# The last network's second quarter by seven block products, and a weight conversion whose stores and refills leave its list of steps

## The chip, the core and the metric

The kernel runs on one core of a Trainium2 chip. Its metric is the device time of one execution in microseconds, the median of several. A core has five engines with queues of their own: PE (TensorE, matrix products), DVE (VectorE), ACT (ScalarE), POOL (GpSimd) and SP (SyncE, which here only issues transfers). Each engine runs its own instructions strictly in the order in which they were recorded, and waits for another engine only where data or a buffer asks for it. So one instruction that waits holds up everything behind it on its engine.

## The reference, cut to what matters

```python
def reference(**inputs):
    # attention: 2 batches, 8 heads, 576 positions, 64 wide, causal window of 128, ALiBi slopes
    x = attention(q, k, v).reshape(1152, 512)
    # four experts, all dense, weighted by normalised probabilities
    p = domain_probs / (domain_probs.sum(-1, keepdims=True) + 1e-09)
    out = 0
    for e in range(4):                       # w1[e]: 512 x 1024, w2[e]: 1024 x 512
        out += p[:, e:e + 1] * (np.maximum(out_of_attention @ w1[e], 0) @ w2[e])
    # the last network: w_in 512 x 2048 and w_out 2048 x 512, both in float64
    h = np.maximum(out @ w_in, 0)
    return (h * h @ w_out).astype(np.float32)
```

`w_in` and `w_out` come as 64-bit floats, since they are drawn as float32 and multiplied by a float64 number.

## The kernel before, in words

**Arithmetic.** A value is kept as a rounded high part and a low part, the remainder, and a product of two such values is three matmuls (high by high, high by low, low by high). ACT makes the high parts by a copy, POOL or DVE the low parts by a subtraction (`rest`, L498 to L500).

**Networks.** The work is a sequence of six networks of 1024 hidden features: `e` = 0 to 3 are the experts (networks 1 to 4 in the text), `e` = 4 and 5 are the two halves of the last network. Each has four weight quarters `g` of 256 hidden features. The second half of `e` = 4, quarters 2 and 3, is the second quarter of the last network.

**Two forms of the first layer.** The plain form (`gemm1`) takes one feature tile `f` of 128 for a chunk of 384 tokens in 12 matmuls; four of them are followed by the second layer (`gemm2`) of that chunk. It is used by `e` = 0 and, before the change, by all of `e` = 4. The block form (`gemm1_pair`, L995 to L1120) takes a whole quarter: weights and tokens are cut into 2 x 2 blocks, and the four blocks of the result come from seven block products instead of eight, each of 2 x 3 matmuls, so 42 matmuls an item. Its token pairs are 2 x 256 (a narrow item, tokens 0 to 511) and 2 x 320 (a wide item, tokens 512 to 1151). Each half of a network runs narrow, narrow, wide, wide: two quarters for the first token pair, then for the second. The second layer of an item runs after the first layer of the next.

**Inside an item.** Three banks `pa`, `pb`, `pc` take the seven products. ACT copies `pa` to `p1` and `pc` to `p5`. DVE adds `u2 = pb + p1` after the second product and `u3 = pb + p1` after the fifth; both are called `u` in the trace, and the fifth and seventh products add into `pb` and so wait for them. DVE and ACT then make the four result blocks `c`, their high and low parts `hmem`.

**Forms.** The block form needs sums of blocks. For weights (`w_forms`, L342) POOL makes four sums (`wsum`, L356), three low parts of blocks (`la`) and four of sums (`ls`), 11 operations, where the plain form (`w_ops`) needs four (`wl`). For tokens (`x_forms`) DVE adds `fxwork` sums (L972).

**Results.** The second layer collects in up to five banks `yacc`. In networks 2 to 4 DVE adds each, scaled by a probability, to `y` (`evac`, L1182); a tile takes one DVE operation. After network 4, PE transposes the nine `y` tiles into the tokens of the last network (`to_x2`).

**Conversion.** DVE and ACT turn the 64-bit weights into 32-bit ones (`convert`, L226 to L312), in 32 halves. A half `j` has an ACT step (`begin`, L271) and four on DVE: a clamp (L277), a shift (L284) and two joins (L291). It works in one of two places `raw` and one of two halves of `both`; `swap` stores a finished half to DRAM (L251) and `reload` fills its place again (L239), both on ACT's queue and, before the change, both steps of the same list, in fixed positions.

**What sets the order.** The code is recorded in the order written. Between the products and tiles it calls `fill(share, us, need)` (L1323 on), which advances a planned clock and lets background steps in: token forms, up to three conversion steps, and weight steps by a quota. A conversion step on DVE goes in only if its planned end lies within `need` of the clock (`spare`), and a running allowance `conv_due` limits their number. So `need` is the opening that DVE's planned work may fill at that place. `want` forces what is overdue.

## Time and profile before

| | |
|---|---|
| median of 3 runs | 670.93 us (670.90 to 671.08) |
| profiled execution | 671.51 us |
| its span, first to last instruction | 669.7 us |
| PE busy | 657.0 us, 98% of the span |
| DVE, ACT, POOL busy | 473.1, 314.8, 395.6 us |
| granted PE clock, mean | 0.995 of full |

The span lies inside the profiled execution's own time, with 1.8 us around it; that execution took 0.58 us longer than the median. Attention and the first network fill the first 183 us, networks 2 to 4 run until about 461 us and the last one until the end. PE's busy time counts overlapping matmuls once; the start-to-start distance of matmuls, and not the duration of one, tells how fast they go.

### The profile page before, as it was taken

Reading aid. Unit: us, or ns where it says so; the run is one execution under the profiler, and the core shown is the slowest. Engines: PE = TensorE matmul, PEld = TensorE weight load, DVE = VectorE, ACT = ScalarE, POOL = GpSimd, SP = SyncE. Lnnn points to the kernel's source line nnn. Section 1 sums busy time; section 2 is a strip of 40 time slices with the busy share of each in tenths; the row PEclk is TensorE's granted clock in tenths of the full one; section 3 lists DMA queues with packets and bytes.
Section 4 is the critical chain, followed back from the end, with each engine's and each line's share of the span. In section 5 each row is a group of like instructions: output and inputs, shape, how many; then the busy total and the mean of one; then the engine's idle time right before and its main releaser. Section 6 shows DMA issues by size and latency. Waiting matters only on the chain.

```text
span 669.7 us, 10853 instructions
## 1 busy us (share of the span) xinstructions
PE 657.0 (98%) x3864; PEld 586.1 (88%) x3864; DVE 473.1 (71%) x982; ACT 314.8 (47%) x761; POOL 395.6 (59%) x473
## 2 busy tenths in 40 slices
PE   7999999999999999999999999999999999999997
PEld 6767888888989899898999989898999999898996
DVE  4787888847888777777877876876668744545453
ACT  5798888623435434333443343433464634333120
POOL 3799996526957744653654664231458984856321
PEclk8999999999999999999999999999999999999999
DMA  7943222011413443444345245354222001100012
GB/s 208 270 121 98 65 73 74 11 64 31 158 32 110 122 142 117 140 127 142 127 125 156 81 134 182 102 181 134 72 95 79 1 0 64 64 0 1 1 64 78
DMA packets 44023, 64.42 MB, mean 96 GB/s; under 512 B 4161, under 2 KB 26177, under 8 KB 43969
## 3 DMA queue, kind: packets, MB, share of 16 engines
q1 hardware_dynamic: 33248, 39.61, 19.4%
q10 hardware_dynamic: 10720, 24.12, 11.9%
q8 instruction: 30, 0.49, 0.3%
q14 instruction: 25, 0.20, 0.1%
HBM read 52.97 MB, written 10.75 MB: 95 GB/s over the span
## 4 chain that ended last, share of the span: by engine, by line
PE 91%; POOL 3%; DVE 2%; ACT 2%; SPq 1%; DMA 1%; issue 1%; POOLq 0%; ACTq 0%
PE yacc L1128 29%; PE hps L1050 26%; PE hps L936 14%; PE yacc L1163 13%; PE xps L731 3%; PE tp L859 2%; PE sc L811 2%; POOL wl L500 1%; PE hps L1575 1%; POOL ts L847 1%; DMA pt<-in_probs_dram 1%; SPq L1399 1%; POOL vl L500 1%; PE xtp L1198 1%; DVE fxwork L972 1%
## 5 line engine op out<-in xcount | busy, mean ns | idle before, releaser
L1128 PE MATMUL yacc<-wh,hmem 128*128 128x512 f32 x576 | 183.7, 390 | 0.0
L500 POOL TENSOR_TENSOR wl<-wraw,wh 128x256 fp32r<-128x256 f32 (+1 forms) x110 | 107.5, 1002 | 63.7 <-ACT wh L433 51.2
L1128 PEld LDWEIGHTS yacc<-wh,hmem 128*128 128x128 f32 x576 | 108.2, 188 | 21.8
L1128 PE MATMUL yacc<-wl,hmem 128*128 128x512 f32 x288 | 112.3, 390 | 0.0
L1163 PE MATMUL yacc<-wh,hmem 128*128 128x512 f32 x272 | 89.2, 393 | 0.0
L500 POOL TENSOR_TENSOR ls<-wsum,hs 128x256 fp32r<-128x256 f32 x64 | 54.5, 879 | 48.1 <-ACT hs L380 47.5
L1061 ACT ACTIVATE p<-hps 128x256 f32<-128x256 f32 (+1 forms) x64 | 26.3, 411 | 98.9 <-PE hps L1050 98.4
L936 PE MATMUL hps<-xh,wh 128*128 128x384 f32 (+1 forms) x208 | 67.1, 323 | 0.0
L936 PE MATMUL hps<-xh,wl 128*128 128x384 f32 (+1 forms) x208 | 65.5, 315 | 0.0
L936 PE MATMUL hps<-xl,wh 128*128 128x384 f32 (+1 forms) x208 | 65.4, 314 | 0.0
L1065 DVE TENSOR_TENSOR u<-hps,p 128x256 f32<-128x256 f32 (+1 forms) x64 | 29.1, 455 | 50.1 <-PE hps L1050 50.0
L1128 PEld LDWEIGHTS yacc<-wl,hmem 128*128 128x128 f32 x288 | 54.1, 188 | 9.9
L1163 PEld LDWEIGHTS yacc<-wh,hmem 128*128 128x128 f32 x272 | 51.0, 188 | 10.4
L291 DVE SCALAR_TENSOR_TENSOR wconv<-wraw,wconv 128x512 int32<-128x512 int32 x64 | 57.2, 894 | 1.3
L1085 ACT ACTIVATE hmem<-c 128x256 fp32r<-128x256 f32 (+1 forms) x72 | 31.0, 445 | 54.1 <-DVE c L1065 52.8
L847 POOL TENSOR_SCALAR ts<-ts,st 128x256 f32<-128x256 f32 (+2 forms) x80 | 40.6, 523 | 26.5 <-DVE st L842 12.3
L500 POOL TENSOR_TENSOR la<-wraw,ha 128x256 fp32r<-128x256 f32 x48 | 44.4, 950 | 19.7 <-ACT ha L366 19.7
L1163 PE MATMUL yacc<-wl,hmem 128*128 128x512 f32 x136 | 53.2, 391 | 0.0
L500 POOL TENSOR_TENSOR hmem<-c,hmem 128x256 fp32r<-128x256 f32 (+1 forms) x32 | 26.9, 861 | 38.3 <-ACT hmem L1081 38.3
L500 POOL TENSOR_TENSOR hmem<-r,hmem 128x384 fp32r<-128x384 f32 x24 | 26.2, 1094 | 39.0 <-ACT hmem L1150 39.0
L1086 DVE SCALAR_TENSOR_TENSOR hmem<-c,hmem 128x256 fp32r<-128x256 f32 (+1 forms) x72 | 38.6, 556 | 14.5 <-ACT hmem L1085 13.0
L832 ACT ACTIVATE ts<-ts,st 128x256 f32<-128x256 f32 (+2 forms) x80 | 37.2, 467 | 12.0 <-DVE st L823 12.0
(141 smaller groups left out, 1743.3 us busy)
## 6 DMA issues: line engine op xcount, KB each, us to landing
wraw<-in_w_dram SPq DMA_DIRECT2D x32, 512.0 KB, 4.1
wraw<-in_w_out_dram ACTq DMA_DIRECT2D x16, 512.0 KB, 3.8
w<-wconv ACTq DMA_DIRECT2D x32, 256.0 KB, 4.0
wraw<-w SPq DMA_DIRECT2D x16, 512.0 KB, 3.5
wraw<-in_w_in_dram ACTq DMA_DIRECT2D x14, 512.0 KB, 3.9
rq<-in_qT_dram SPq DMA_DIRECT2D x8, 256.0 KB, 7.1
out_dram<-y SPq DMA_DIRECT2D x8, 256.0 KB, 2.3
rk<-in_kT_dram SPq DMA_DIRECT2D x8, 192.0 KB, 5.7
```

Of the source, the lines that this page charges most:

```text
L291: nc.vector.scalar_tensor_tensor(out=ai, in0=raw[j][:, :, part], scalar=amount, in1=ai, op0=op, op1=ALU.bitwise_or,)
L500: e.tensor_tensor(out=out, in0=in0, in1=f32(in1), op=ALU.subtract)
L832: nc.scalar.activation(out=ts[0:n, g, :], in_=ts[0:n, g, :], func=ACTF.Exp, bias=st[0:n, 0, g:g + 1], scale=-1.0, accum_out=st[0:n, 1, g:g ...
L847: nc.gpsimd.tensor_scalar(out=ts[0:n, g, :], in0=ts[0:n, g, :], scalar1=st[0:n, 2, g:g + 1], scalar2=1.0, op0=ALU.mult, op1=ALU.mult,)
L936: nc.tensor.matmul(out=ps, lhsT=l_[:, k, cs], rhs=r_[:, k, cols], start=(k == 0 and r_ is xh and l_ is wh and not second), stop=(k == KT - ...
L1050: nc.tensor.matmul(out=ps, lhsT=a[l_][:, k, :], rhs=b[r_][:, k, :], start=start and k == 0 and l_ == r_, stop=stop and k == 1 and l_ == 1, ...
L1061: nc.scalar.activation(out=out, in_=x, func=ACTF.Copy)
L1065: nc.vector.tensor_tensor(out=out, in0=x, in1=y, op=ALU.add)
L1085: nc.scalar.activation(out=hh, in_=src, func=ACTF.Relu)
L1086: nc.vector.scalar_tensor_tensor(out=hl, in0=src, scalar=0.0, in1=f32(hh), op0=ALU.max, op1=ALU.subtract)
L1128: nc.tensor.matmul(out=y, lhsT=l_[:, ns], rhs=r_[:, fo, :], start=(first and fo == 0 and j == 0), stop=(last and fo == FTQ - 1 and j == 2),)
L1163: nc.tensor.matmul(out=y, lhsT=l_[:, ns], rhs=r_[:, fo, :], start=(first and j == 0), stop=(last and j == 2),)
```

## The change

Quarters 2 and 3 of `e` = 4 go by the block form: 4 items of 42 matmuls take the place of 12 feature tiles of 12, and their weights get block forms on POOL. Their results are added to `y` by DVE (`fresh` is true only for the first half). Token forms of the last network are made in two steps, the first pair's as soon as its tokens are there, and `run_x2` is called twice where it was called once. The conversion's store and refill become one step `move` in a list of its own, `moves`: it is entered when the second join is recorded, and each `fill` tries its head once. Conversion no longer runs beside the token forms of the last network. The allowance falls from 0.85 to 0.7 steps a us, while most openings `need` grow.

```diff
-        def swap(j):
+        def move(j):
             i, h = todo[j]
             if not by(at["out", j]):
                 return False
...
             nc.scalar.dma_start(out=single[i][:, h * n:(h + 1) * n], in_=both[:, j % 2, :])
             at["gone", j] = clock["now"] + 5.0
             if h:
                 stored.add(i)
-
-        def reload(j):
-            if not by(at["out", j]):
-                return False
-            load(j + 2, nc.scalar)
+            if j + 2 < len(todo):
+                load(j + 2, nc.scalar)
...
-                at["out", j] = clock["DVE"] + 0.5
+                if part == 0:
+                    at["out", j] = clock["DVE"] + 0.5
+                    moves.append(lambda: move(j))
...
@@ gemm1_pair @@
         add(u2, pb, p1)
-        fill(0.6, step, 1.8)
+        fill(0.6, step, 2.1)
...
         copy(p5, pc)
-        fill(0.6, step, 1.1)
+        fill(0.6, step, 1.5)
...
-        fill(0.6, step, 0.8 + 1.4 * (2 * n // P))
+        fill(0.6, step, 1.5 + 1.4 * (2 * n // P))
@@ evac @@
-            if e == 0 or (e == E and f < FT // 2):
+            fresh = e == E and f < (NQ if two else FT) // 2
+            if e == 0 or fresh:
@@ items @@
-            if e == E:
+            if (e, r) == (E, 0):
@@ flush_one @@
-            need = 0.8 + (1.38 - 0.74 * last) * i if two else 3.0 + 0.69 * i
+            need = 1.5 + (1.38 - 0.74 * last) * i if two else 3.0 + 0.69 * i
@@ fill @@
-        conv_due[0] = min(conv_due[0] + 0.85 * us, 12.0)
+        conv_due[0] = min(conv_due[0] + 0.7 * us, 12.0)
         given = False
+        if moves and moves[0]() is not False:
+            moves.pop(0)
         for _ in range(3):
-            if conv and need and (x_late or not xbg) and conv_due[0] >= 1.0 and conv[0]() is not False:
+            if conv and need and not xbg and conv_due[0] >= 1.0 and conv[0]() is not False:
@@ pace @@
-        return max(most * step, len(bg) / 2)
+        return max(most * step, len(bg) / (1 if wnext["ops"] == len(order) else 2))
@@ main loop @@
         if e >= E and (ch or f):
             run_x2("y")
+            run_x2("y")
```

The DVE order before, at the second narrow item of network 4's first half: the end of the item ahead, the five `y` tiles of the second layer between, `u` of the item, and what follows it. `wconv` rows are the conversion's clamp, shift and joins in turn.

```order
L1086 SCALAR_TENSOR_TENSOR hmem<-c_4385,hmem 128x256
L1182 SCALAR_TENSOR_TENSOR y<-yacc,pt,y 128x512 x2
L277 TENSOR_SCALAR wconv<-wconv 128x512
L284 TENSOR_SCALAR wconv<-wconv 128x512
L1182 SCALAR_TENSOR_TENSOR y<-yacc,pt,y 128x512 x3
L1065 TENSOR_TENSOR u_4508<-hps,p_4506 128x256
L291 SCALAR_TENSOR_TENSOR wconv<-wraw_2390,wconv 128x512 x2
L1086 SCALAR_TENSOR_TENSOR hmem<-hps,hmem 128x256
```

The same place now.

```order
L1089 SCALAR_TENSOR_TENSOR hmem<-c_4402,hmem 128x256
L1186 SCALAR_TENSOR_TENSOR y<-yacc,pt,y 128x512
L278 TENSOR_SCALAR wconv<-wconv 128x512
L285 TENSOR_SCALAR wconv<-wconv 128x512
L292 SCALAR_TENSOR_TENSOR wconv<-wraw_2391,wconv 128x512
L1186 SCALAR_TENSOR_TENSOR y<-yacc,pt,y 128x512
L292 SCALAR_TENSOR_TENSOR wconv<-wraw_2391,wconv 128x512
L1186 SCALAR_TENSOR_TENSOR y<-yacc,pt,y 128x512 x3
L1068 TENSOR_TENSOR u_4534<-hps,p_4532 128x256
L278 TENSOR_SCALAR wconv<-wconv 128x512
L285 TENSOR_SCALAR wconv<-wconv 128x512
L1089 SCALAR_TENSOR_TENSOR hmem<-hps,hmem 128x256
```

Two joins now stand among the `y` tiles, ahead of `u`; behind `u` a clamp and a shift have taken the place of two joins.

The ACT order before, at the first narrow item of the same half: `p_4379` and `p_4380` are `p1` and `p5`, `wh` the high parts of a weight.

```order
L239 DMA wraw_2390<-in_w_out_dram 128x512
L271 ACTIVATE wconv<-wraw_2391 128x512
L251 DMA w_4360<-wconv 128x512
L433 ACTIVATE wh<-wraw 128x512 x2
L1061 ACTIVATE p_4379<-hps 128x256
L1061 ACTIVATE p_4380<-hps 128x256
L1085 ACTIVATE hmem<-hps 128x256
```

The same place now.

```order
L251 DMA w_4316<-wconv 128x512
L239 DMA wraw_2391<-in_w_in_dram 128x2x256
L1064 ACTIVATE p_4396<-hps 128x256
L251 DMA w_4420<-wconv 128x512
L239 DMA wraw_2390<-in_w_out_dram 128x512
L436 ACTIVATE wh<-wraw 128x512 x2
L1064 ACTIVATE p_4397<-hps 128x256
L1088 ACTIVATE hmem<-hps 128x256
```

A store, a refill and the two `wh` copies have moved in between `p1` and `p5`.

The POOL order before, at the start of the last network: `hmem` are the low parts of a chunk's four feature tiles.

```order
L500 TENSOR_TENSOR wl<-wraw,wh 128x256 x20
L500 TENSOR_TENSOR hmem<-r,hmem 128x384 x4
L500 TENSOR_TENSOR wl<-wraw,wh 128x256 x7
L500 TENSOR_TENSOR hmem<-r,hmem 128x384 x2
L500 TENSOR_TENSOR wl<-wraw,wh 128x256
L500 TENSOR_TENSOR hmem<-r,hmem 128x384 x2
```

The same place now, from the second chunk's last low part to the last chunk's first.

```order
L503 TENSOR_TENSOR hmem<-r,hmem 128x384
L359 TENSOR_TENSOR wsum<-wraw,wsum 128x256
L503 TENSOR_TENSOR la<-wraw,ha 128x256 x3
L503 TENSOR_TENSOR ls<-wsum,hs 128x256 x4
L503 TENSOR_TENSOR wl<-wraw,wh 128x256 x2
L503 TENSOR_TENSOR hmem<-r,hmem 128x384
```

Ten weight operations now stand ahead of the last chunk's first low part; before, there were seven `wl` ahead of the second chunk's and seven ahead of the third's.

## Rows read from the trace of the kernel before

**Rows 1.** Busy us by stretch (instructions): PE, PEld, DVE, ACT, POOL; clock, DMA, GB/s.
```profile
183.00:454.00 271.00, 270.79 (x1586) 245.84 (x1587) 209.92 (x376) 109.03 (x233) 143.61 (x165) 1.00 0.40 125
470.00:516.00 46.00, 46.00 (x248) 42.44 (x247) 32.26 (x44) 25.73 (x51) 27.75 (x28) 1.00 0.22 70
```

**Rows 2.** Chain that ended last: start us, us, what, instructions.
```profile
367.00 5.11 PE hps L1050 x42
372.12 6.83 PE yacc L1128 x30
...
384.06 5.45 PE yacc L1128 x24
389.50 6.16 PE hps L1050 x42
...
505.27 8.34 PE hps L936 x48
513.61 8.20 PE yacc L1163 x36
```

**Rows 3.** Timeline of DVE, a wide item: start us, us, what.
```profile
215.43 0.47 DVE L1065 TENSOR_TENSOR u<-hps,p 128x320 f32<-128x320 f32 x1
```

**Rows 4.** Timeline of PE, that item's fifth product.
```profile
215.98 0.40 PE L1050 MATMUL hps<-xh,hs 128*128 128x320 f32 x1
```

**Rows 5.** Timeline of PE, second narrow item of network 4.
```profile
378.78 0.28 PE L1050 MATMUL hps<-xh,ha 128*128 128x256 f32 x1
...
381.65 0.28 PE L1050 MATMUL hps<-xh,hs 128*128 128x256 f32 x1
...
383.09 0.38 PE L1050 MATMUL hps<-hm,ha 128*128 128x256 f32 x1
```

**Rows 6.** Timeline of DVE, narrow items of network 4; in brackets idle before.
```profile
366.60 1.11 DVE L291 SCALAR_TENSOR_TENSOR wconv<-wraw,wconv 128x512 int32<-128x512 int32 x1
...
368.89 0.68 DVE L291 SCALAR_TENSOR_TENSOR wconv<-wraw,wconv 128x512 int32<-128x512 int32 x1
...
375.35 1.40 DVE L1182 SCALAR_TENSOR_TENSOR y<-yacc,pt,y 128x512 f32<-128x512 f32 x2
376.67 0.45 DVE L277 TENSOR_SCALAR wconv<-wconv 128x512 f32<-128x512 f32 x1
377.14 0.85 DVE L284 TENSOR_SCALAR wconv<-wconv 128x512 int32<-128x512 int32 x1
377.91 2.06 DVE L1182 SCALAR_TENSOR_TENSOR y<-yacc,pt,y 128x512 f32<-128x512 f32 x3
380.48 0.42 DVE L1065 TENSOR_TENSOR u<-hps,p 128x256 f32<-128x256 f32 x1 [0.51 <-PE hps L1050]
380.82 1.41 DVE L291 SCALAR_TENSOR_TENSOR wconv<-wraw,wconv 128x512 int32<-128x512 int32 x2
```

**Rows 7.** Timeline of POOL, the same stretch.
```profile
366.25 3.92 POOL L500 TENSOR_TENSOR wl<-wraw,wh 128x256 fp32r<-128x256 f32 x4 [4.49 <-ACT wh L433]
370.24 0.74 POOL L356 TENSOR_TENSOR wsum<-wraw 128x256 f32<-128x256 f32 x1
...
373.33 2.68 POOL L500 TENSOR_TENSOR la<-wraw,ha 128x256 fp32r<-128x256 f32 x3
```

**Rows 8.** Timeline of ACT, first narrow item of network 4.
```profile
365.55 1.14 ACT L433 ACTIVATE wh<-wraw 128x512 fp32r<-128x512 f32 x2
367.81 0.39 ACT L1061 ACTIVATE p<-hps 128x256 f32<-128x256 f32 x1 [1.12 <-PE hps L1050]
369.25 0.39 ACT L1061 ACTIVATE p<-hps 128x256 f32<-128x256 f32 x1 [1.05 <-PE hps L1050]
369.91 0.38 ACT L1085 ACTIVATE hmem<-hps 128x256 fp32r<-128x256 f32 x1 [0.28 <-PE hps L1050]
...
374.16 0.36 ACTq L251 DMA_DIRECT2D w<-wconv  x1
```

**Rows 9.** Timeline of POOL, last network.
```profile
500.93 7.55 POOL L500 TENSOR_TENSOR wl<-wraw,wh 128x256 fp32r<-128x256 f32 x7
```

55 lines of the change are left out of this document (31 added, 24 removed).

## The prediction

> **What bounds the kernel now.** The page comes first: PE, the tensor engine, is busy for 98% of the span. Then the busy time by stretch: from 183 to 454 us, which is networks 2 to 4, PE works 270.79 of 271.00 us, and from 470 to 516 us, the start of the last network, 46.00 of 46.00, at the full granted clock [rows 1]. The reader is to see that no wait is left there: work taken from PE shortens the kernel, a new wait lengthens it, and no wait can be won back (0.21 us at most). Third, the chain that ended last: past 183 us it is PE alone, blocks of 42 matmuls (first layer by seven products) and of 24 or 30 (second layer) in turn [rows 2].
>
> What can stop PE is read from the timelines. The fifth product of an item adds into the bank that DVE's first `u` reads. In a wide item of network 2 `u` runs from 215.43 to 215.90 and the product's first matmul starts at 215.98, 0.08 later [rows 3, 4]. In a second narrow item of network 4 there is room: `u` ends at 380.90, the fifth product starts at 381.65 [rows 5, 6]. The seventh product waits for the second `u` in the same way, and there is no room: its first matmul takes 0.38 us where the others take 0.28 [rows 5].
>
> **The change part by part.** *Fewer products.* Four feature tiles of 3 chunks go: 3 x 8.34 = 25.02 us. In come two quarters of a narrow and a wide item: 2 x (5.11 + 6.16) = 22.54 [rows 2]. That is -2.48. The second layer is 3 x 8.20 = 24.60 before and 2 x (5.45 + 6.83) = 24.56 after: -0.04. The nine transposes only pair up: 0. Saved: 2.52 us, all on the bounding engine. The gain is 10% of the first layer and not an eighth because short matmuls are dearer by the column: 8.34/48 = 0.174 us for 384 columns, 5.11/42 = 0.122 for 256. The Trainium skill (TensorE: Matmul & The Clock Gate, Back-to-back issue gap) gives columns over 2.4 plus 2.5 ns, by which the saving would be an estimated 2.8 us and the sum below 0.3 lower; the rows have 12 ns more for each matmul, and they decide.
>
> *Conversion moved on DVE.* This hides behind nothing, because PE has no slack. In a second narrow item DVE evacuates five `y` tiles before `u`. Before, a clamp and a shift stand among them; now a clamp, a shift and two joins, and the clamp and shift that follow `u` take the place of two joins. From 375.35 the old five `y`, clamp and shift take 1.32 + 0.47 + 0.77 + 2.06 = 4.62 us, then DVE idles 0.51 until `u` at 380.48 [rows 6]. A join takes 0.68 us alone and 1.11 with POOL at work [rows 6, 7]. POOL is at work here: 366.25 to 376 without a gap, and later after the change, as its low parts wait for ACT copies that now come after the first narrow item's `p`. I take one join of each: `u` starts at 375.35 + 4.62 + 1.79 = 381.76, 1.28 late, ends at 382.18, and the fifth product starts at 382.26 instead of 381.65: 0.61 lost. Behind `u`, clamp and shift take 0.9 (unslowed; an estimate, twice 0.45) to 1.24, where the joins took 1.45 from 380.82 until the next operation, so the second `u` is late by 1.28 + 1.05 - 1.45 = 0.88, and the seventh product with it. That second lateness contains the first. Price of one place: 0.85 us; bounds 0.3 (both joins 0.68, slowed clamp and shift absent) and 1.5 (both 1.11).
>
> The order has this in both halves of network 3 and the first of network 4. In the first of these half of POOL's low parts come early, so I take the low end there: 0.3 + 2 x 0.85 = 2.0 (0.9 to 4.5). In network 2's second half a join more stands behind `u`: 1.5 (1.0 to 2.6). In network 4's second half POOL builds no forms, but the extra join is there: 0.5 (0 to 1.5). Sum 4.0, bounds 1.9 and 8.6. First narrow items lose the join behind their `u`, wide ones mostly swap like for like: 0.
>
> *Stores and refills in a list.* Each half store still goes on ACT's queue, now with its refill. In three first narrow items (network 3's second half, both of network 4) store, refill and the two `wh` copies stand between the first `p` and the second. Two issues at 0.36 and 1.14 of copies put the second `p` at 367.81 + 0.72 + 1.14 = 369.67 (0.39 more if nothing overlaps) instead of 369.25, and the rounding behind it at 370.06 to 370.45 instead of 369.91 [rows 8]. That rounding leads to the second `u`: 0.15 to 0.54 each. What waits behind it is the DVE remainder, then PE. I take 0.2 each, 0.6 together. In network 2's second half two `ha` copies (768 columns, 0.86 by the `wh` row) come before it: 0.4. Sum 1.0, bounds 0 and 2.2.
>
> *Last network.* POOL now makes block forms for two more weights: 30 weight operations stand among the 12 remainders (`hmem`) from 470 to 516 us, ten ahead of the first remainder of the last chunk. One takes 0.74 alone and 7.55/7 = 1.08 beside DVE's forms [rows 7, 9]. With 12 remainders at about 0.99 (27.75 us for 28 operations, [rows 1]) that is 34 to 44 of 46 us. It fits, with little room: 0.4, bounds 0 and 3. DVE's token forms come earlier, but DVE was busy 32.26 of 46 there [rows 1] and conversion has left the stretch: 0. The last quarters run as before, 0.
>
> Sum: -2.52 + 4.0 + 1.0 + 0.4 = +2.9. On the profiled execution of 671.51 that is 674.4; the runs' median lies 0.58 lower, 670.93, so 673.8. With every added term at its low bound it would be 670.3, with all at the high one 682.
>
> **The rivals.** *The openings hold.* If POOL is idle while DVE evacuates, shift and joins run unslowed: 375.35 + 3.38 + 0.9 + 1.36 = 380.99, `u` is 0.5 late, clamp and shift of 0.9 fit where 1.45 was, and nothing is lost. It decides at 0.67 us of lateness at the fifth product, or where lateness and clamp and shift together pass 1.45. For it: POOL is busy only 143.61 of 271 us [rows 1]. Against it: its operations come in one run that covers this place [rows 7]. ACT's delays would then be lost in the idle time too: 670.93 - 2.52 = 668.4.
>
> *Loss and gain cancel.* Terms near their low bounds, about 2.5 us: 671. For it: four of five places may meet POOL for a part only.
>
> *POOL bounds the last network.* The ten weight operations, slowed to 1.4 where I count 1.08 (an estimate, a third above rows 9), delay the remainder that the second layer needs right after the last chunk's first layer. For it: POOL has that little room; against it: rows 9 show seven in a row at 1.08. 3 us on top: 676.8.
>
> *Every join waits out a POOL operation.* A join then takes 0.68 + 0.98 (3.92/4, [rows 7]), two of them 3.32; `u` is 2.81 late and the second `u` 2.81 + 1.24 - 1.45 = 2.6, so the three like places cost 7.8 instead of 2.0: 679.6. Against it: the join of 366.60, with POOL at work throughout, took 1.11 [rows 6, 7]. The Trainium skill (SBUF — State Buffer, SBUF: two separate sides) states it as a rule: the port that DVE and GpSimd share is an exclusive lock, and the loser blocks for the whole instruction. By that row the trace agrees on the contention, not on its full length.
>
> **How the numbers follow.** Forecast 673.8 (672.3 to 676): 0.46. The openings hold, 668.4: 0.24. Cancel, 671: 0.17. POOL bounds, 676.8: 0.09. Whole waits, 679.6: 0.04. The measurement tells 0.2%, 1.3 us, from no change. Slower: 0.46 + 0.09 + 0.04 = 0.59, less a rest of the forecast that falls inside, 0.58; same 0.18; faster 0.24. The range has to take in the openings' case and POOL's, not the last: 668.3 to 677.0. The likeliest case's own is 672.3 to 676.
>
> **What would show it.** The last network's first layer has four blocks of 42 in place of the last twelve of 12, 22.5 us: right saving. In networks 2 to 4 PE's waits on DVE's `u` come to some 4 us, and blocks of 42 in second narrow items grow from 5.11 to about 6: forecast. PE busy still 270 of 271 there: the openings hold. PE waiting on POOL `hmem` between 500 and 520 us: the last rival. The forecast is wrong if DVE idles before `u` in second narrow items as it does now.

## The result and the profile after

The changed kernel takes 679.97 us (median of 4 runs, 679.82 to 680.59) beside 671.0 us (670.9 to 671.68) for the kernel before in the same session: ratio 1.0133, interval 1.0116 to 1.0151. It is 1.3% slower, by 8.97 us. The forecast was 673.8 us, slower by 2.9, and its range ended at 677.0: the sign was right, the size three times too small.

The profiled execution of after took 679.89 us, its span is 678.1. Attention and the first network differ between profiles of nearly equal code by up to 1.2 us (the first item of network 2 starts at 177.78 us before, at 176.98 after, at 176.62 to 177.63 in the experiments), so what follows compares lengths inside the later networks, not clock times. By these, networks 2 to 4 are 7.2 us longer and the last network is 2.0 us longer where 2.5 were to be saved, that is 4.5 lost.

The busy time by stretch, in the columns of [rows 1]:

```profile
183.00:454.00 271.00, 267.95 (x1541) 239.49 (x1540) 215.93 (x383) 107.48 (x234) 130.64 (x163) 1.00 0.42 136
470.00:516.00 46.00, 46.00 (x241) 41.58 (x240) 34.90 (x40) 22.53 (x44) 32.06 (x29) 1.00 0.04 13
500.00:520.00 20.00, 20.00 (x104) 18.18 (x104) 16.48 (x18) 11.20 (x23) 19.84 (x18) 1.00 0.15 52
```

PE (first figure after the length) idles 3.05 us of 271 in networks 2 to 4, where it idled 0.21. That is less than half of the 7.2 us. Matmuls start 0.12 us apart and are shown at 0.28, so the record of the one ahead covers the first 0.16 us of a wait; and one that had to wait is itself shown at 0.38 or 0.39 us, with the next one 0.22 behind it. Some 0.26 us of each wait do not show, and one of under 0.16 us does not show at all. In 470 to 516 PE looks as busy as before, while POOL (last busy figure) has gone from 27.75 to 32.06, and to 19.84 of 20 us from 500 on. What PE waited for, from 183 to 660 us (us in total, times, longest); the kernel before has one such wait, of 0.3 us:

```profile
PE hps L1053 <- ACT p L1064: 2.5, 6, 1.1
PE hps L1053 <- DVE u L1068: 1.6, 4, 0.7
PE yacc L1166 <- POOL hmem L503: 1.4, 1, 1.4
```

Three engines hold PE back where there was one. Together the waits show 5.5 us of the 11.7 lost, for the same reason; the distance from the first matmul of a block to the first of the next has all of it. By that distance, items of 42 matmuls lose against the kernel before:

```
                     first narrow   second narrow   wide (net 2, first half)
network 2, 2nd half      0.37           0.92             0.63
network 3, 1st half      1.41           0.61             -
network 3, 2nd half      0.50           0.72             -
network 4, 1st half      0.52           0.73             -
network 4, 2nd half      0.53           0.06             -
sum                      3.33           3.04             0.63
```

*Second narrow items.* Three different things hold them. First PE, in the second narrow item of network 4's first half (answering to [rows 5]), then DVE ahead of and in it (answering to [rows 6]):

```profile
383.79 0.28 PE L1053 MATMUL hps<-xh,ha 128*128 128x256 f32 x1
...
387.32 0.39 PE L1053 MATMUL hps<-xh,hs 128*128 128x256 f32 x1
...
388.84 0.35 PE L1053 MATMUL hps<-hm,ha 128*128 128x256 f32 x1
```

```profile
380.01 0.74 DVE L1186 SCALAR_TENSOR_TENSOR y<-yacc,pt,y 128x512 f32<-128x512 f32 x1
380.67 1.00 DVE L278 TENSOR_SCALAR wconv<-wconv 128x512 f32<-128x512 f32 x1
381.70 0.84 DVE L285 TENSOR_SCALAR wconv<-wconv 128x512 int32<-128x512 int32 x1
382.58 1.11 DVE L292 SCALAR_TENSOR_TENSOR wconv<-wraw,wconv 128x512 int32<-128x512 int32 x1
383.61 0.74 DVE L1186 SCALAR_TENSOR_TENSOR y<-yacc,pt,y 128x512 f32<-128x512 f32 x1
384.27 0.68 DVE L292 SCALAR_TENSOR_TENSOR wconv<-wraw,wconv 128x512 int32<-128x512 int32 x1
384.87 2.06 DVE L1186 SCALAR_TENSOR_TENSOR y<-yacc,pt,y 128x512 f32<-128x512 f32 x3
386.85 0.41 DVE L1068 TENSOR_TENSOR u<-hps,p 128x256 f32<-128x256 f32 x1
```

DVE no longer idles before `u`. `u` starts 3.06 us into the item where it started 1.70 in: 1.36 late. One join takes 1.11 us beside POOL's `la` (380.65 to 383.14) and one 0.68 after it. The fifth product starts 3.53 us in instead of 2.87, the seventh 5.05 instead of 4.31. PE also waits 0.17 us for a `p` there, at 386.28, but without the store that holds this `p` (e4 below) the item loses 0.85 all the same. The like item of network 3's second half has the same order and loses 0.72.

In network 3's first half the order on DVE is the same, but what ends last is ACT's `p`, behind a store and a refill. PE, at the fourth product:

```profile
289.82 0.39 PE L1053 MATMUL hps<-xh,ha 128*128 128x256 f32 x1 [0.34 <-ACT p L1064]
```

In network 2's second half `u` is not late: it starts 1.70 us into the item, which begins at 237.65, and DVE idles before it as in the kernel before. Clamp and shift behind it run beside POOL's `ls` and take twice their time, so that the second `u`, and the seventh product with it, are late. DVE, POOL, PE:

```profile
239.35 0.42 DVE L1068 TENSOR_TENSOR u<-hps,p 128x256 f32<-128x256 f32 x1 [0.75 <-PE hps L1053]
239.69 0.84 DVE L278 TENSOR_SCALAR wconv<-wconv 128x512 f32<-128x512 f32 x1
240.57 0.85 DVE L285 TENSOR_SCALAR wconv<-wconv 128x512 int32<-128x512 int32 x1
238.13 3.00 POOL L503 TENSOR_TENSOR ls<-wsum,hs 128x256 fp32r<-128x256 f32 x4 [6.32 <-ACT hs L383]
242.86 0.39 PE L1053 MATMUL hps<-hm,ha 128*128 128x256 f32 x1 [0.74 <-DVE u L1068]
```

POOL starts `ls` there because ACT's `hs` copies stand behind a store that DVE's join releases at 236.44.

*First narrow items.* ACT, then DVE, in the first narrow item of network 4's first half (371.34 us on), answering to [rows 8]:

```profile
372.25 0.38 ACT L1064 ACTIVATE p<-hps 128x256 f32<-128x256 f32 x1 [4.32 <-PE hps L1053]
372.75 0.33 ACTq L251 DMA_DIRECT2D w<-wconv  x1
373.17 0.40 ACTq L239 DMA_DIRECT2D wraw<-in_w_out_dram  x1
373.61 1.15 ACT L436 ACTIVATE wh<-wraw 128x512 fp32r<-128x512 f32 x2 [0.98 <-DVE u L1068]
374.67 0.36 ACT L1064 ACTIVATE p<-hps 128x256 f32<-128x256 f32 x1
374.94 0.37 ACT L1088 ACTIVATE hmem<-hps 128x256 fp32r<-128x256 f32 x1
```

```profile
375.34 0.42 DVE L1089 SCALAR_TENSOR_TENSOR hmem<-hps,hmem 128x256 fp32r<-128x256 f32 x1 [1.87 <-ACT hmem L1088]
375.68 0.41 DVE L1068 TENSOR_TENSOR u<-hps,p 128x256 f32<-128x256 f32 x1
```

Between the two `p` stand store, refill and two `wh` copies, one after the other; the store starts only at 372.75, when DVE's join has ended (372.72). The rounding is at 3.60 us of the item where it was at 3.07, DVE stands idle for 1.87 us, and the seventh product is late by just that half microsecond.

*Last network.* POOL, then PE, where the last chunk's remainders lie (answering to [rows 9]):

```profile
518.74 1.88 POOL L503 TENSOR_TENSOR wl<-wraw,wh 128x256 fp32r<-128x256 f32 x2
520.58 1.57 POOL L503 TENSOR_TENSOR hmem<-r,hmem 128x384 fp32r<-128x384 f32 x1
522.11 0.73 POOL L503 TENSOR_TENSOR wl<-wraw,wh 128x256 fp32r<-128x256 f32 x1
522.81 1.02 POOL L503 TENSOR_TENSOR hmem<-r,hmem 128x384 fp32r<-128x384 f32 x1
523.79 1.31 POOL L503 TENSOR_TENSOR wl<-wraw,wh 128x256 fp32r<-128x256 f32 x1
525.07 2.54 POOL L503 TENSOR_TENSOR hmem<-r,hmem 128x384 fp32r<-128x384 f32 x2
```

```profile
522.21 0.72 PE L1166 MATMUL yacc<-wh,hmem 128*128 128x512 f32 x2 [1.44 <-POOL hmem L503]
...
527.31 0.39 PE L1053 MATMUL hps<-xh,ha 128*128 128x256 f32 x1 [1.08 <-ACT p L1064]
...
528.68 0.39 PE L1053 MATMUL hps<-xh,hs 128*128 128x256 f32 x1 [0.40 <-DVE u L1068]
```

The last chunk's first remainder `hmem` had its input from ACT at 518.40, but stood behind two `wl` until 520.58; it ended at 522.15, and PE's second layer took it at 522.21. The ten weight operations ahead of it ran almost without a gap from 509.95, 1.06 us each. The next item then takes 7.07 us for 5.09, since the late remainders push ACT's copies and roundings and DVE's `u` too, and a wide one 6.63 for 6.15. The block form itself does what it should: all other items of the new half take 5.09 to 5.10 and 6.16 to 6.17.

### The profile page after: what moved, and what is told of

It is laid out like the page before. It is cut to its first block, busy times and chain, and to the rows that moved or that the text cites. A ratio compares the mean times of both kernels' runs of the same rounds, so it can differ in the third digit from the quotient of the medians.

```text
span 678.1 us, 10945 instructions
## 1 busy us (share of the span) xinstructions
PE 661.7 (98%) x3888; PEld 585.8 (86%) x3888; DVE 487.8 (72%) x1006; ACT 313.7 (46%) x769; POOL 399.1 (59%) x491
## 4 chain that ended last, share of the span: by engine, by line
PE 65%; DVE 14%; POOL 9%; ACT 5%; issue 3%; ACTq 1%; SPq 1%; DMA 1%; POOLq 0%; DVEq 0%
PE yacc L1131 24%; PE hps L1053 20%; PE hps L939 7%; PE yacc L1166 5%; DVE wconv L292 3%; DVE hmem L1089 3%; PE xps L734 3%; POOL wl L503 2%; PE tp L862 2%; POOL hmem L503 2%; DVE c L1068 2%; PE sc L814 2%; POOL wsum L359 1%; DVE y L1186 1%; POOL ls L503 1%
## 5 line engine op out<-in xcount | busy, mean ns | idle before, releaser
L503 POOL TENSOR_TENSOR wl<-wraw,wh 128x256 fp32r<-128x256 f32 (+1 forms) x102 | 90.8, 914 | 83.7 <-ACT wh L436 50.3
L1131 PE MATMUL yacc<-wl,hmem 128*128 128x512 f32 x324 | 126.5, 390 | 0.0
L503 POOL TENSOR_TENSOR hmem<-c,hmem 128x256 fp32r<-128x256 f32 (+1 forms) x48 | 42.1, 892 | 52.1 <-ACT hmem L1084 52.1
L939 PE MATMUL hps<-xh,wh 128*128 128x256 f32 (+1 forms) x160 | 50.9, 318 | 0.0
L292 DVE SCALAR_TENSOR_TENSOR wconv<-wraw,wconv 128x512 int32<-128x512 int32 x64 | 48.6, 759 | 1.6
L939 PE MATMUL hps<-xh,wl 128*128 128x256 f32 (+1 forms) x160 | 49.4, 309 | 0.0
L939 PE MATMUL hps<-xl,wh 128*128 128x256 f32 (+1 forms) x160 | 49.3, 308 | 0.0
L1053 PE MATMUL hps<-xh,hs 128*128 128x256 f32 (+1 forms) x144 | 43.6, 303 | 1.5 <-DVE u L1068 0.8
L1053 PE MATMUL hps<-xh,ha 128*128 128x256 f32 (+1 forms) x144 | 42.9, 298 | 2.0 <-ACT p L1064 2.0
L1053 PE MATMUL hps<-lt,hs 128*128 128x256 f32 (+1 forms) x144 | 42.6, 296 | 0.0
```

What stands on the lines that cost most here:

```text
L292: nc.vector.scalar_tensor_tensor(out=ai, in0=raw[j][:, :, part], scalar=amount, in1=ai, op0=op, op1=ALU.bitwise_or,)
L503: e.tensor_tensor(out=out, in0=in0, in1=f32(in1), op=ALU.subtract)
L939: nc.tensor.matmul(out=ps, lhsT=l_[:, k, cs], rhs=r_[:, k, cols], start=(k == 0 and r_ is xh and l_ is wh and not second), stop=(k == KT - ...
L1053: nc.tensor.matmul(out=ps, lhsT=a[l_][:, k, :], rhs=b[r_][:, k, :], start=start and k == 0 and l_ == r_, stop=stop and k == 1 and l_ == 1, ...
L1131: nc.tensor.matmul(out=y, lhsT=l_[:, ns], rhs=r_[:, fo, :], start=(first and fo == 0 and j == 0), stop=(last and fo == FTQ - 1 and j == 2),)
```

## The experiments

All times are medians beside runs of the kernel before on the same chip, with the ratio's interval. The lengths (us against the kernel before, from each run's one profile) are:

```
run                      first   second  wide,    last      median   ratio to before
                         narrow  narrow  nets2-4  network
changed kernel            3.33    3.04    0.7     +2.0      679.97   1.0133 [1.0116, 1.0151]
e1_plain_second           2.94    3.36    0.7      0.0      677.86   1.0103 [1.0088, 1.0118]
e2_block_only             0       0       0       +7.8      679.15   1.0124 [1.0109, 1.0139]
e3_old_openings           1.52    0.05    0.6     +1.4      674.82   1.0053 [1.0036, 1.0070]
e4_stores_on_sp           0.46    1.96    0.7     +1.9      676.37   1.0079 [1.0064, 1.0094]
e5_wide_forms_later       3.22    3.03    0.7     +3.6      681.08   1.0148 [1.0131, 1.0165]
e6_weights_later          3.37    3.30    0.7     -2.5      675.74   1.0071 [1.0056, 1.0086]
e7_both_later             3.12    3.40    0.7     +1.0      678.73   1.0108 [1.0091, 1.0124]
e8_combined               1.77    0.02    0.6     +1.5      673.77   1.0044 [1.0029, 1.0059]
e9_sp_and_weights         0.46    2.01    0.8     -2.6      671.55   1.0010 [1.0001, 1.0019]
e10_three_moves           1.77    0.03    0.6     -0.2      673.36   1.0033 [1.0021, 1.0046]
e11_four_moves            0.02    0.03    0.5     -0.2      671.14   1.0002 [0.9993, 1.0011]
e12_weights_not_held      0       0       0.5     -1.0      670.36   0.9991 [0.9982, 1.0000]
e13_order_of_change       0.01    3.29    0.7     -2.7      671.77   1.0012 [1.0003, 1.0020]
e14_conversion_last       0.01    0.02    0.5     +0.4      671.60   1.0005 [0.9996, 1.0014]
e15_one_join_less         0       0.01    0       +0.3      670.93   0.9996 [0.9988, 1.0005]
e16_conversion_spread     0       0       0       +3.9      674.54   1.0051 [1.0037, 1.0065]
e17_spread_further        0       0       0       -0.5      670.53   0.9997 [0.9988, 1.0006]
e18_load_landed           0       0.02    0       -2.6      668.16   0.9952 [0.9938, 0.9965]
```

The first narrow item of network 2 has no column: from e11 on it is 0.4 us shorter than in the kernel before. The time lay in the range of the stated theory in e1, e9 and e18; it was better than the theory in e3, e4 and e6, and worse in the others, mostly because a loss moved on to another item.

Each diff is against the changed kernel, or the run that it names.

**Which part costs what: e1, e2, e3.** e1 takes the block form back out of the last network's second quarter and leaves list and openings:

```
-            fresh = e == E and f < (NQ if two else FT) // 2
+            fresh = e == E and f < FT // 2
-            if (e, r) == (E, 0):
+            if e == E:
...
```

> The changed kernel with the last network's second quarter left in the plain form (12 feature tiles of 12 matmuls), all else of the change kept: conversion list, openings, allowance, token forms in two steps. Theory (two separate losses: 7.1 us in networks 2 to 4 from the conversion's new places on DVE and ACT, 4.5 us in the last network from POOL, which only the block form's weight sums bring): 671.0 + 7.1 = 677 to 678 us, blocks of 42 in networks 2 to 4 as long as in the changed kernel, no wait of PE on POOL past 500 us. Rival (the last network's loss comes from the token forms that now stand earlier and without gaps on DVE): PE still waits on POOL or ACT between 500 and 550 us, 680 to 682 us.

Measured 677.86. Networks 2 to 4 lose what they lose in the changed kernel, the last network nothing. So the conversion's new order (list, openings and allowance together) costs some 7 us by itself, and the block form, instead of its 2.5 us of gain, adds 2.1.

e2 does the reverse, block form alone with the old list of stores and refills, the old openings and the old rate of conversion:

```
-        fill(0.6, step, 2.1)
+        fill(0.6, step, 1.8)
-        fill(0.6, step, 1.5)
+        fill(0.6, step, 1.1)
-        conv_due[0] = min(conv_due[0] + 0.7 * us, 12.0)
+        conv_due[0] = min(conv_due[0] + 0.85 * us, 12.0)
...
-                    moves.append(lambda: move(j))
...
+                ops.insert(1, lambda: swap(j - 1))
```

> The block form and the token forms in two steps as in the changed kernel, but the conversion with the list, the openings and the allowance of before, so that DVE and ACT have the order of before through networks 2 to 4. Theory (the last network's loss is POOL's and DVE's load there, whatever the conversion does before): networks 2 to 4 as before, blocks of 42 at 5.11 and 6.16, then -2.5 saved and 4.5 or more lost in the last network, where the conversion's last steps now stand too: 673 to 676 us. Rival (the loss there is made by the conversion's new places alone): 668.5 us.

Neither: 679.15, and not a microsecond of it in networks 2 to 4, whose items are those of the kernel before. One item of the last network takes 15.42 us. ACT there, and PE:

```profile
519.20 0.74 ACT L1002 ACTIVATE hm<-fxwork 128x640 fp32r<-128x640 f32 x1 [3.36 <-DVE fxwork L971]
524.30 0.63 ACT L1002 ACTIVATE xh<-fxwork 128x512 fp32r<-128x512 f32 x1 [4.37 <-DVE fxwork L971]
524.84 0.36 ACT L1060 ACTIVATE p<-hps 128x256 f32<-128x256 f32 x1
```

```profile
525.26 0.58 PE L1049 MATMUL hps<-xh,ha 128*128 128x256 f32 x1 [8.37 <-ACT p L1060]
```

A `p` stands behind ACT's rounding of a token form, which waits for DVE; DVE's forms of the second wide chunk stand packed ahead of that item, because it now comes earlier and because 11 us of conversion steps still stand among the forms from 478 to 506 us. So block form and conversion's order belong together: faster conversion was the way to clear the start of the last network, and it is where the price is paid.

e3 keeps list and block form and puts back only the old openings and rate (the first six lines of e2's diff, and 0.8 for 1.5 in the openings after the last product and among the `y`).

> The changed kernel with the openings 1.8, 1.1, 0.8 and 0.8 and the allowance 0.85 of before; list, block form and token forms as changed. In its order one join, not two, stands among the y tiles of second narrow items and the store behind u; but clamp, shift and two joins stand ahead of u in first narrow items. Theory (what counts is what stands ahead of u and of p on DVE and ACT, item by item): second narrow items lose 0.2 instead of 0.7, first narrow ones 0.5 to 1.4 each, 678 to 681 us. Rival (the wider openings are the cause of the loss in networks 2 to 4): 671.0 - 2.5 + 4.5 = 673 us.

674.82, so my expectation fell and the rival was nearer. With one join less among the five `y` the second narrow items lose nothing at all (5.11 to 5.13). The wider openings, or the lower allowance that was put back with them, are the cost there, and not the list by itself. But the store also moves behind `u` in e3; join and store are told apart by e4, e9 and e10. Four first narrow items still lose 0.38 each, and the last network 3.9: conversion is not done when it starts, a shift and a join stand ahead of an `u` for which PE waits 1.99 us, and PE's granted clock falls behind that wait (0.51 from 524 to 526 us).

**The stores on ACT, and the joins: e4, e13, e15.** e4 issues stores and refills on SP's queue:

```
-            nc.scalar.dma_start(out=single[i][:, h * n:(h + 1) * n], in_=both[:, j % 2, :])
+            nc.sync.dma_start(out=single[i][:, h * n:(h + 1) * n], in_=both[:, j % 2, :])
-                load(j + 2, nc.scalar)
+                load(j + 2, nc.sync)
```

> The changed kernel with the conversion's stores and refills issued on SP's queue instead of ACT's; DVE's and POOL's order is unchanged. Theory (in first narrow items store, refill and two wh copies hold the second p; in second narrow items DVE's u is late by itself, and p behind the store is hidden under it): first narrow items go from 0.5 lost to 0.1, second narrow ones keep 0.7: 677 to 678 us. Rival (p behind a store that waits for its join is what costs both kinds of items): about 674.5 us. If SP's weight loads then wait behind a store, POOL is late and it gains nothing: 680 us or more.

676.37, between the two. First narrow items lose 0.46 in all instead of 3.33, network 3's first one 0 instead of 1.41: what they lost was ACT's place in line. In second narrow items DVE's order is as it was, yet network 2's second half now loses 0.07 instead of 0.92 and network 3's first half 0 instead of 0.61: half of what these items lost was the stores' too. The other two still lose 0.85 and 0.86; there DVE's own order is the cause.

e13 moves POOL's work against DVE's conversion, without any change in what is done: on top of e9 (below), no weight operation is put between the second `p` and the first rounding of an item in networks 2 to 4:

```
-        fill(0.6, step, 1.5)
+        fill(0.6, step, 1.5, e >= E)
...
-        while quota["left"] >= 1.0 and not given:
+        while quota["left"] >= 1.0 and not given and bg_too:
```

> The changed kernel's openings, with stores and refills on SP's queue, the fourth quarter's weight operations behind the last chunk's remainders, and no weight operation between the second p and the first rounding in networks 2 to 4. The conversion ends before the last network. Theory (in two second narrow items POOL's operations slow DVE while two joins stand ahead of u, 0.85 us each; they stay): 671.5 - 0.45 = 670.8 to 671.2 us. Rival (the low parts come later, so POOL rests while DVE works on the y tiles, and the two items lose nothing): 669.3 to 669.6 us.

671.77. Two second narrow items now lose 1.58 us each where they lost 0.87. The same join in the same item, in e9 and then in e13; and in e13 what POOL does beside it:

```profile
333.32 0.68 DVE L292 SCALAR_TENSOR_TENSOR wconv<-wraw,wconv 128x512 int32<-128x512 int32 x1
```

```profile
332.32 1.27 DVE L292 SCALAR_TENSOR_TENSOR wconv<-wraw,wconv 128x512 int32<-128x512 int32 x1
```

```profile
330.27 2.77 POOL L503 TENSOR_TENSOR la<-wraw,ha 128x256 fp32r<-128x256 f32 x3
```

With POOL's `la` beside it the join takes nearly twice as long. A place's price depends on what POOL does at that moment, as [rows 6, 7] had it.

e15 takes one join out of the one wide item that loses, by a narrower opening there alone, on top of e14 (below):

```
-        fill(0.6, step, 1.5, e >= E)
+        fill(0.6, step, 1.5 if (e, ch, g) != (1, 1, 1) else 0.5, e >= E)
```

> As e14_conversion_last, and in one place, the second wide item of network 2's first half, the opening behind the second p is 0.5 instead of 1.5, so that the join that stood between u and DVE's remainder moves behind the item. Theory (clamp, shift and join behind u, 1.5 us, make the second u late there and nothing else does): that item goes from 6.85 to 6.25 us, 0.6 us less than e14_conversion_last: 667.9 to 668.4 us. Rival (the join then stands ahead of y tiles and costs in the next items): no gain.

That item goes from 6.85 to 6.30, and the items of networks 2 to 4 now lose nothing beyond 0.1 us in all. The time, 670.93, is 0.67 less than e14's but not the 667.9 to 668.4 expected, since e14 itself had come out higher. The join at 215.97 of the changed kernel, ahead of the second `u`, was the cause.

**The last network: e5, e6, e7.** e6 lets the work on the fourth quarter's weight (15 operations on POOL, and their copies on ACT) begin only behind the last chunk's remainders. e5 leaves the weights and holds the last token forms of the second wide chunk (three sums, a copy, a low part) back until the first narrow item is recorded. e7 does both. The edit of e6, then that of e5:

```
+                if order[i][:2] == (E, NQ // 2 + 1) and not plain_over[0]:
+                    return False
                 w_start()
...
+            plain_over[0] = (e, ch, f) == (E, len(CHUNKS) - 1, FT // 2 - 1)
```

```
+        late_ok = lambda: wide_soon[0]
...
-            t3[:3] + [held(t3[3]), t3[4]],
+            [held(t3[0], late_ok) if eng == "LATE" else t3[0]] + t3[1:3] + [held(t3[3]), t3[4]],
...
             h = gemm1_pair(e, ch, f)
+            wide_soon[0] = e == E
```

> The changed kernel with one step of the last network moved: the wide pair's last token forms (three sums, a copy, a low part) are recorded after the last network's first narrow item instead of ahead of it. Order of POOL unchanged. Theory (the block form needs the token forms 38 us earlier, and the wide pair's last ones stand on DVE ahead of u and on ACT ahead of p of the first narrow item): that item goes from 7.07 to 5.1 to 5.5 us, PE's wait of 1.6 us on POOL's remainder stays: 678.0 to 678.5 us. Rival (POOL's load alone bounds there): under 0.5 us gained, 679.5 us or more.

> The changed kernel with another step moved: the weight operations of the last network's fourth quarter (15 on POOL, and their copies on ACT) start only behind the last chunk's remainders instead of ahead of them. Order of DVE unchanged. Theory (POOL stands late before that chunk's remainders because of these): the waits of 1.6 and 0.3 us on POOL go, and DVE is slowed less, so the first narrow item's 2.0 us lost shrink to 0.5 to 2: 676.5 to 678 us. Rival (the weight operations are then late for the second narrow item): 1 us or more lost there, 679 to 680 us.

> The changed kernel with both moves: wide pair's last token forms behind the first narrow item, fourth quarter's weight operations behind the last chunk's remainders. Theory (together they are the whole loss of the last network, 4.5 us): 680.0 - 4.0 = 675.5 to 676.5 us, blocks of 42 in the last network at 5.1 and 6.2 us, networks 2 to 4 as in the changed kernel. Rival (the loss only moves on, to the second narrow item or the second layer): 678 us or more.

e6: 675.74, and the last network is 2.52 us shorter than before, the whole of the saving. POOL by stretch and by operation:

```profile
500.00:520.00 20.00, 20.00 (x106) 18.56 (x105) 16.41 (x23) 10.12 (x20) 8.92 (x8) 1.00 0.08 27
```

```profile
516.39 1.02 POOL L503 TENSOR_TENSOR hmem<-r,hmem 128x384 fp32r<-128x384 f32 x1 [8.83 <-ACT hmem L1153]
```

POOL is busy 8.92 us of 20 instead of 19.84, waits for each remainder instead of being waited for, and PE waits for nothing from 480 us on. So the weight operations among the remainders were all of the 4.5 us, ACT's and DVE's late work included; POOL's operations and their copies on ACT moved together, so their shares are not told apart. DVE's token forms beside POOL's operations were longer as well: the six that follow each other from 509.15 us on take 8.2 us in the changed kernel, and 4.5 (from 509.14) in e6. e5 moves the loss on: the first narrow item falls from 7.07 to 5.75, a wide one rises to 9.72. e7 is worse than e6, since with DVE's form out of the way POOL's order shifts once more and an item of 8.65 waits 1.9 us for `ls`, and PE's granted clock falls behind that wait (0.52 from 537 to 540 us).

**Adding up: e8 to e12, e14.** e9 is e4 and e6 together. e8 is e4, e7 and the old opening of 0.8 among the `y`. e10 is e9 with that opening, and conversion held from the start of the last network until after its second narrow item. e11 adds the edit of e13 to e10. e12 is e11 and lets a weight operation follow a conversion step at once in the last network. e14 is e12 with conversion held until after the second wide item (1 for 0 in the last condition):

```
-            need = 1.5 + (1.38 - 0.74 * last) * i if two else 3.0 + 0.69 * i
+            need = 0.8 + (1.38 - 0.74 * last) * i if two else 3.0 + 0.69 * i
...
-            if conv and need and not xbg and conv_due[0] >= 1.0 and conv[0]() is not False:
+            if conv and need and not xbg and not conv_off[0] and conv_due[0] >= 1.0 and conv[0]() is not False:
...
-                given = True
+                given = not in_last[0]
...
+            if (e, ch, f) == (E, 0, NQ // 2 + 1):
+                conv_off[0] = False
```

> Four edits on the changed kernel together: both moves in the last network, stores and refills on SP's queue, and the opening between y tiles at 0.8 as before (so that one join and not two stands ahead of u in second narrow items). Three conversion halves are then left for the last network, behind its first narrow item. Theory (losses in networks 2 to 4 and in the last network are separate and each has its own cause): networks 2 to 4 lose 0.6 to 1.5 instead of 7.1 us, the last network 0 to 1 instead of 4.5, the saving of 2.5 stays: 669.5 to 671.5 us. Rival (the three halves left cost in the last network what they no longer cost before it): 673 us or more.

> The changed kernel with two of the moves: stores and refills on SP's queue, and the fourth quarter's weight operations behind the last chunk's remainders; openings as in the change. Theory (the two causes add): 671.0 - 2.5 + 3.1 (networks 2 to 4 as measured with the stores on SP) + 0 to 0.5 = 671.5 to 672.5 us. Rival (a part of the gain of either was the other's): 673.5 us or more.

> The changed kernel with stores and refills on SP's queue, the opening between y tiles at 0.8, the fourth quarter's weight operations behind the last chunk's remainders, and the three conversion halves that are left behind the last network's second narrow item; the wide pair's token forms stay where the change put them. Theory: networks 2 to 4 lose 2.4 us (0.62 in one wide item, 0.44 in each of four first narrow items, where two copies stand ahead of the first rounding on ACT), the last network 0 to 0.7: 671.0 - 2.5 + 2.4 + 0.3 = 670.9 to 671.6 us. Rival (the three halves left cost 1 us or more in the last network): 672.5 us.

> As the one before, and in networks 2 to 4 no weight operation is let in between the second p and the first rounding, so the two copies on ACT stand behind that rounding. DVE and POOL keep their order. Theory (those copies alone hold the first rounding, DVE's remainder, the second u and with it the seventh product): first narrow items lose 0 instead of 0.44, networks 2 to 4 lose 0.6 in all: 669.2 to 670 us, faster than the kernel before. Rival (the low parts that wait for those copies come later and slow DVE in second narrow items): no gain, 671 us.

> As the kernel with four moves, and in the last network a conversion step no longer keeps a weight operation out of the same opening. DVE's order changes in two rows; POOL's low parts of the next quarter stand earlier. Theory (the 2.2 us that the last network still loses there, 1.67 of them in the second narrow item of the network's second half, come from weight operations that the three conversion halves left in it push back, so that PE waits 1.4 us for a low part on POOL): that wait goes, 668.8 to 669.3 us, faster than the kernel before by 0.25 to 0.3%. Rival (the conversion's DVE and ACT work itself costs there): under 0.7 us gained, 670.5 us or more.

> As the one with weight operations not held back, but the three conversion halves that are left go behind the last network's second wide item instead of its second narrow one; POOL's order is unchanged. Theory (the 1.7 us that the first wide item of the last network lost there came from the conversion beside POOL's sums, for which two copies on ACT ahead of p1 wait): that item goes from 7.88 to 6.2 us, 670.4 - 1.7 = 668.5 to 669 us. Rival (the loss moves on to the items where the conversion now stands): 670 us or more.

e9 gives 671.55: the gains of e4 (3.6 us) and e6 (4.2) make 7.8 together, and 8.4 is found, within the intervals; so the two causes are separate. With the opening of 0.8 there is one join less ahead of `u` in second narrow items, with the stores on SP in both runs: e9 loses 0.87 in each of two, e10 nothing. But with that opening (e8, e10, e11) conversion runs late into the last network and each way of placing the rest there moves the loss: items of 8.72 (e8), 6.76 (e10, e11), 7.88 (e12) and 7.81 (e14) in turn. At none of the places tried did conversion, packed closely, go into the last network without a wait.

**Conversion spread thin: e16, e17, e18.** e16 is e15 with conversion let in again from behind the second narrow item on, but paced in the last network (0.25 steps per us instead of 0.7) and with none between the two `u` of an item. e17 paces at 0.2. e18 is e16 with POOL's and ACT's work on a converted weight recorded only 14 us after its store:

```
-        fill(0.6, step, 2.1)
+        fill(0.6, step, 2.1 if e < E else 0.0)
...
-        conv_due[0] = min(conv_due[0] + 0.7 * us, 12.0)
+        conv_due[0] = 0.0 if conv_off[0] else min(conv_due[0] + (0.25 if in_last[0] else 0.7) * us, 12.0)
```

```
+                landed[i] = clock["now"] + 14.0
...
+                if in_last[0] and clock["now"] < landed.get(i, 0.0):
+                    return False
```

> As e15_one_join_less, but the 15 conversion steps that are left start behind the last network's second narrow item, at most 0.25 of them a us instead of 0.7 (and without the allowance that had gathered), and none between the two u of an item. Theory (it was not the conversion's amount that cost 1.7 and 2.7 us there but its coming in one run beside POOL's sums, ahead of u): the last network's items stay at 5.1 and 6.2 us, 670.9 - 2.9 = 668.0 to 668.5 us, faster than the kernel before by 0.35 to 0.45%. Rival (any conversion there costs what it cost, 0.7 us a half): 670 us or more.

> As e16_conversion_spread with 0.2 steps a us. Theory: the same, 668.0 to 668.5 us, unless the weights that are converted last then come late for the end of the last network: 669 us or more.

> The kernel of the run with conversion spread over the last network (0.25 steps per us), with one edit: the copies and forms made from a converted weight in the last network are put into their lists only 14 us after that weight's store is recorded, where before they followed at the next free place. In that run ACT's wh copies stood ahead of a p and waited 7.82 us for the load, so one item of 42 matmuls took 11.60 us where 5.09 is its length; every other item lost nothing except one of 6.28 for 6.25. My theory: the wait for the load was the whole of what was lost, and the load has landed by then. The items at 607 and 619 us take 5.09 and 5.10, PE waits for no p there, and the time is 674.54 - 6.5 = 668.0 (667.6 to 668.8), which is the kernel before less the 2.5 us of products saved. Rival: the copies come too late for the last second layer or stand ahead of another p, or POOL's forms of that weight, now closer to the end, hold the remainders: the loss moves on by 1.5 to 3 us, 669.5 to 671, with a long item at 630 us or a wait at the last second layer.

In e16 every item has its length but one of 11.60 us, near the end. ACT there:

```profile
613.03 1.15 ACT L436 ACTIVATE wh<-wraw 128x512 fp32r<-128x512 f32 x2 [7.82 <-DMA wraw<-w]
614.08 0.64 ACT L1064 ACTIVATE p<-hps 128x256 f32<-128x256 f32 x2
```

The load of the converted weight was issued at 609.69; the copies that need it stood in ACT's line ahead of two `p`. e17 has the same at another place (2.16 us lost at 630). e18 moves only those copies and the forms made from them:

```profile
620.99 0.39 ACT L1065 ACTIVATE p<-hps 128x256 f32<-128x256 f32 x1 [4.80 <-PE hps L1054]
621.27 0.62 ACT L437 ACTIVATE wh<-wraw 128x512 fp32r<-128x512 f32 x1
622.43 0.39 ACT L1065 ACTIVATE p<-hps 128x256 f32<-128x256 f32 x1 [0.54 <-PE hps L1054]
```

```profile
500.00:650.00 150.00, 150.00 (x880) 136.96 (x879) 92.17 (x159) 59.72 (x132) 101.11 (x125) 1.00 0.14 46
```

No `p` is held, PE works 150.00 of 150.00 us, and the last network is 2.57 us shorter than in the kernel before. e18 takes 668.16 us, faster than both kernels: 0.9952 [0.9938, 0.9965] of the kernel before. Some 0.4 us more comes from the first narrow item of network 2 (5.84 instead of 6.26), which e13's edit shortens.

## Why the prediction was wrong, point by point

- *The saving, -2.52 us: right.* The last network is 212.96 us long in e6 and 212.90 in e18, where it was 215.48.
- *Second narrow items, +4.0: the sum near, +3.04, the mechanism right for half of it.* In two of the three like places the working holds step by step: `u` 1.36 us late (1.28 forecast), one join at 1.11 and one at 0.68 as assumed, the fifth product 0.66 late (0.61), the item 0.72 and 0.73 longer (0.85). e9 and e10 show it: a join less, no loss. The third, network 3's first half (0.61, forecast 0.3), waits for a `p` behind a store. In network 2's second half (0.92, below my low bound of 1.0) DVE idles before `u`, the sign that I had named against the forecast, and the loss is made behind `u`, beside an `ls` that the store's place on ACT had put there. With the stores on SP (e4) these two places lose 0.07 together. Network 4's second half lost 0.06 (0.5). So 1.5 of the 3.04 belongs to the stores, which I had not counted in these items, and that the sum came near is luck. One row was misread as well: the join of 0.68 at 368.89 ran beside POOL's `wl` [rows 6, 7]; 0.68 is nevertheless what a join takes alone (two of them 1.41 at 380.82).
- *First narrow items, under stores and refills, +1.0: the step that failed in size, +3.33.* Two things were wrong. I let store, refill and copies overlap with the first `p`, and took 0.2 of the 0.15 to 0.54; nothing overlaps, so the three places cost 0.50 to 0.53, the upper end. And I gave network 3's first half nothing: there two stores and two refills stand on ACT ahead of the first and the second `p`, each store behind a join of DVE, and it costs 1.41. e4 shows both, with 0.46 left of 3.33.
- *Wide items, "swap like for like: 0": wrong by 0.63 in one place*, a join ahead of the second `u`; e15 shows it.
- *Last network, +0.4 with a bound of 3: the step that failed most, +4.5.* The price of an operation was right (1.08 forecast, 1.06 measured). But the estimate compared POOL's work with the whole stretch, 34 to 44 of 46 us, and called that room. PE does not wait for the stretch's sum; it waits for a given remainder, and what counts is the weight operations that stand ahead of that one. From 500 on POOL was busy 19.84 of 20 us. The rival had this mechanism, though only for operations slowed to 1.4 us, and gave it 3 us on top of the 0.4, with a chance of 0.09; its sign, PE waiting for `hmem`, is there at 522.21. It left out that late remainders push ACT's roundings and `p` and DVE's `u` of the next item, 2.5 us of the 4.5. e6 shows that all of it hangs on where that weight's operations stand.
- *The rivals.* "The openings hold" falls with DVE's missing idle time in the three like places, "cancel" with 11.7 us lost against 2.5 gained. "Every join waits out a POOL operation" had 679.6, nearest to the measured time, but by a mechanism that is not there: joins beside POOL took 1.11 to 1.27 us and not 1.66, and second narrow items lost 3.0, not 9.8 as it would have them. Its number is met by three other sums.
- *Range.* It ended at the POOL rival's time, with the other terms at their likely values. What came was that case, a third larger (4.5 for 3.4), together with first narrow items above the bound of 2.2 that I had given them. In the terms of the sum: -2.52 + 3.04 + 3.33 + 0.7 + 4.5 = +9.05, where the medians have 8.97.

What stays open: why DVE's clamp, shift and join take up to 2.4 times as long beside some POOL operations and less beside others was not tried apart, and neither were the wider openings and the lower allowance. e18's gain was measured as a whole; whether the old list of stores with spread conversion would do as well was not tried.

## What to carry to other kernels

An engine with room by the sum of a stretch can still be late for one instruction: count what stands ahead of the one that is waited for, in its line, and not the stretch. Whatever is put into the line of an engine that feeds the bound one (a DMA issue that waits for another engine's result, a copy that waits for a load) holds back everything behind it, so place it behind the instruction that the bound engine needs, or on another queue. When work that was hidden is made denser to clear a place, look at what it is beside on the way: here spreading it thinner and giving its load time to land was what let the saving show.

## What the runs showed of the hardware

Short waits of PE hide in its busy time: 11.7 us of longer blocks appear as 5.5 us of waits, since matmuls that start 0.12 us apart are shown at 0.28, and one that starts after a wait at 0.38 to 0.39.

DVE's operations are lengthened, not blocked for a whole POOL operation, when POOL works beside them: clamp 0.41 to 0.84 or 1.00, shift 0.43 to 0.84 (once 0.97), join 0.68 to 1.11 or 1.27, while `y` stays at 0.66 to 0.74 and `u` at 0.41 to 0.42. It can go the other way: in the kernel before, the join at 368.89 kept its 0.68 us, and the `wl` that started under it at 368.97 took 1.19 where the one ahead had taken 0.74.

A wait can also cost PE's clock. In e16, around the wait (PE is the first busy figure, the clock the third from the end):

```profile
610.00:613.00 3.00, 0.22 (x2) 0.01 (x1) 0.00 (x0) 0.00 (x0) 1.09 (x2) 0.89 0.53 175
613.00:617.00 4.00, 2.50 (x11) 2.50 (x12) 0.42 (x1) 2.08 (x5) 0.72 (x1) 0.50 0.00 0
617.00:620.00 3.00, 3.00 (x18) 2.91 (x17) 1.98 (x5) 0.62 (x2) 1.25 (x2) 0.64 0.00 0
620.00:626.00 6.00, 6.00 (x28) 4.96 (x27) 4.53 (x8) 0.96 (x3) 4.08 (x6) 1.00 0.01 3
```

The wait of 4.28 us ends at 614.50. Behind it the clock is at its lower level, 1.2 of 2.4 GHz, the item's matmuls start 0.21 us apart instead of 0.12, and the item is 2.2 us longer than the wait that is shown makes it. Waits of 1.75 us in e5, 1.86 in e7, 1.89 in e8, 1.99 in e3 and 8.37 in e2 came with such a fall too; one of 1.90 in e17, those of 1.42 in e10 and e11 and the 1.44 and 1.08 of the changed kernel did not. What decides it is not shown.
